# Where the last two column groups fetch their input rows, and which queue moves them: a state-space convolution block with a gated bilinear network on one core

## The chip, the cores and the metric

One core of one Trainium2 chip runs the kernel. The metric is device time in microseconds (us), from one launch; the figure given is the median of three runs. One further execution of the same program was taken with the hardware profiler on, and every time that is read from a trace below belongs to that one execution.

## The reference

The input x is one sequence of 2048 tokens with 640 features, float32. Cut to what matters:

```python
mod = (silu(c) @ w_mod)                       # sa, ca, ga, sb, cb, gb: six rows of 640
h = layernorm(x) * (1 + ca) + sa
x = x + ga * S4(h)                            # a causal convolution over the 2048 tokens, one filter per feature, by FFT, plus h * Dskip
h = layernorm(x) * (1 + cb) + sb
x = x + gb * (((h @ w_gate) * (h @ w_up)) @ w_down)   # 640 -> 1536 -> 640
```

The filter of a feature is a sum over 192 complex states of C * exp(dt*A*l) * B.

## The kernel before, in words

The 640 features are five column groups of 128 (`db` 0 to 4, `NB` = 5). The 2048 tokens are seen as 128 partitions of 16 tokens, and the 16 are four quarters of four (`c` 0 to 3), so that one token block is 128 x 4 = 512 tokens. The kernel has two parts.

The first part (to about 500 us in the profile) makes the filters (matmuls into the tile `kg`), transforms filters and inputs (`u_k`, `u_pre`, `u_g`), multiplies them in the frequency domain and goes half the way back (`u_c`, which stores its result in the DRAM tensor `WD`, one per column group, through the two buffers `Wa` and `Wb`), and goes the rest of the way back in `u_d`. For one column group and one quarter, `u_d` loads the piece of `WD` into a buffer `TVa` or `TVb` (two transfers of 256 KB) and the input columns of x into a buffer `xsa` or `xsb` (256 KB in runs of 512 bytes), runs four matmuls into a PSUM tile, adds the input to it on VectorE, and stores the sum to the DRAM tensor `x2d` (256 KB). All of these transfers are issued by SyncE (SP), the stores of `WD` at the end by ScalarE.

The second part is the network. It starts with token blocks 0 and 1 (quarters 0 and 1), whose sums are also kept in SBUF, in the tiles `xb0` and `xb1` (128 x 4 x 640, `XB` in the code). `rows` loads columns 0 to 383 of such a block back from `x2d`; for the last two column groups, `u_d` writes its sum straight into the kept tile. `u_head` then takes the statistics of the layernorm (`bn_stats` on VectorE, tile `a`), the factors `hr`, the normalized pieces `hf` (half of each on ScalarE, half on GpSimd), their transposes on TensorE, and the split of these into two float32r parts `hh` and `hl`. From there on the matmuls of the network run (`prod`, the lines of `pa` and `psg`) to the end of the kernel. Thirty and then four matmuls with no use of their result (`warm`) stand where TensorE would have no work ahead of `u_head`.

Every engine works through its own list in order, and so does the list of transfers that an engine issues. The order of the lists is written out: `SCHED` gives, for each step of each job (`d` for `u_d`, `c` for `u_c`, `w` for weight loads, `wl` for `rows`, `h` for `u_head`), a place in one common count from about -1000 to 2880, and `due` runs the steps as the count goes by. A job is a generator; each `yield` ends a step. `SLOT` says by a letter for each allocation which of two or three buffers of a ring (`TV`, `xs`, `hf`, `psf`) it takes. A transfer into a buffer waits until the readers of its former content are done, and each transfer that SP or ScalarE issues also waits for the one that used the same semaphore, eight transfers back.

Of the kernel before, what the change touches and what calls it, by code (L numbers as in the profile page):

```python
# [14 lines left out]
OP = mybir.AluOpType  # L15
# [79 lines left out]
            (2433, 2608, 2608, 2648, 2679, 2703),  # L95
            (2425, 2484, 2537, 2554, 2645, 2677),
            (2477, 2493, 2636, 2656, 2680, 2719),
            (2387, 2439, 2532, 2545, 2620, 2633),
# [48 lines left out]
        (2461, 2497),  # L147
        (2497, 2510),
    ),
    low=(168, 419, 677, 899, 1101, 1385, 1631, 1857, 2075),  # L150
    w=(2478, 2613, 2684, 2668, 2879, 2879),
    wl=(2590, 2441),
    wm=(2732, 2755),
    h=(2709, 2738, 2775, 2811, 2843, 2843, 2857, 2875),
# [6 lines left out]
    ),  # L161
)
# [5 lines left out]
    TV="baabababaabbaabbbabbaababbaababbaabbabbaababab",  # L168
# [3 lines left out]
    hf="abacbcabacbacabcbacccacaabbcbaacabaabbabcaccababbcbbacaabcabbcbba",  # L172
    psf="cacabccbcaccbabbaacbbcacabacbcbacacbbaacabbcabcabcbacbbcbcbcababccbacabcabacbacbaccacbacbaccababbcabcabcabbcabcabcacacab"
    "cbcbaacbacbacbabccabcaacabcaabcbcabcabccabcabcbbacbcbacbacbacbacbacbbabccabacbaacbcabcbacabcabcabcabcababcacbabcacbaacbc"
    "abaabcabcacbacbacacbacbacaaacacbcaba",
    tr="bbababababababababababababababababababababababbabbabababaababbaaababababababababababababababababbbabbababaababababbabbbb"
    "a",
    xs="aabababbabaaabababab",
# [51 lines left out]
def tile_kernel(ctx: ExitStack, tc: tile.TileContext, I, out):  # L230
# [46 lines left out]
    def need(n, *k):  # L277

        assert done.get(k, 0) >= n, k
# [695 lines left out]
    def u_d(db, c):  # L975
        need(4, "WD", db)
        Vt = ring(fp, [P, 2, 4, P], "TV")
        v = WD[db].rearrange("(b t q h) k d -> (q h k) t b d", t=2, q=2, h=2)
        for h in range(2):
            SY.dma_start(Vt[:, h], v[:, h, 4 * c : 4 * c + 4])  # L980
        xs = ring(fp, [P, 4, P], "xs")
        SY.dma_start(xs, xin[:, 4 * c : 4 * c + 4, db * P : db * P + P])
        yield
        d0 = slice(db * P, db * P + P)
        ps = ring(PF[-1], [P, 4, P], "psf")
        for q in range(4):
            lo = q % 2 * 64
            PE.matmul(ps[32 * q : 32 * q + 32], t_ib[lo : lo + 64], Vt[lo : lo + 64, q // 2], start=True, stop=True, tile_position=(lo, 32 * q))
        yield
        mark("d", c)  # L990
        if db >= NB - 2 and c < 2:
            V.tensor_tensor(XB[c][:, :, d0], ps, xs, op=OP.add)
            xs = XB[c][:, :, d0]
        else:
            V.tensor_tensor(xs, ps, xs, op=OP.add)
        SY.dma_start(x2d[:, 4 * c : 4 * c + 4, d0], xs)
# [357 lines left out]
    for t in range(3 * NK + 24):  # L1354
# [17 lines left out]
        if t == 3 * NK + 1:  # L1372
# [519 lines left out]
```

## Time and profile before

| | |
|---|---|
| three runs | 964.3, 961.07, 963.75 us, median 963.75 |
| the profiled execution | 962.34 us, span 960.6 us from its first to its last instruction |
| mean granted TensorE clock | 0.989 |
| busy share of the span | TensorE 93%, VectorE 73%, ScalarE 60%, GpSimd 49% |
| bytes moved | 188.59 MB, 196 GB/s over the span |

The span leaves out 1.74 us of the profiled execution's own time, around the first and the last instruction. In the profile a row of the timeline gives start and length in us, the engine, the source line and the tiles (out<-in); in square brackets stands how long the engine had been idle before the row and what ended that. SPq and ACTq are transfers issued by SyncE and ScalarE; their length is that of the issue, not of the transfer.

### The profile page before, as it was taken

The numbers are of one execution on the slowest core, as the hardware profiler recorded it, in microseconds if no ns is written. First come the engines' busy times: TensorE is split into PE (matmuls) and PEld (weight loads), VectorE is DVE, ScalarE is ACT, GpSimd is POOL, SyncE is SP. The second block draws the span as 40 slices with busy tenths as digits, with TensorE's granted clock in tenths as the row PEclk, the third lists the DMA queues.
The fourth block names the chain that finished last, engine by engine and source line by source line (L and its number), as shares of the span: only waits on it lengthen the run. The fifth ranks groups of instructions, "written<-read, shape, count | busy, mean of one in ns | idle before, by whom it ended". The sixth has DMA issues, their size and how long they took to land.

```text
span 960.6 us, 27559 instructions
## 1 busy us (share of the span) xinstructions
PE 892.6 (93%) x11646; PEld 734.0 (76%) x11646; DVE 705.6 (73%) x1250; ACT 580.5 (60%) x1016; POOL 471.2 (49%) x369
## 2 busy tenths in 40 slices
PE   1898787999899899998889999999999999999998
PEld 1675555878776677887558888889999788888997
DVE  8977888878888986767688555557585766569952
ACT  6989999887988977763276333234463543435430
POOL 3998997986699668750041345320013323231110
PEclk9989999999999999999999999999999999999999
DMA  7876546435267646547894675435536576758875
GB/s 238 324 243 242 186 131 199 146 108 153 78 207 197 187 124 194 184 128 228 277 308 152 192 246 192 165 140 172 200 120 196 171 238 208 244 172 289 253 231 189
DMA packets 158819, 188.59 MB, mean 196 GB/s; under 512 B 9828, under 2 KB 128360, under 8 KB 157544
## 3 DMA queue, kind: packets, MB, share of 16 engines
q1 hardware_dynamic: 149480, 155.51, 50.3%
q0 software_dynamic: 4752, 21.63, 7.8%
q10 hardware_dynamic: 4464, 9.70, 2.7%
q8 instruction: 91, 1.49, 0.6%
q14 instruction: 32, 0.26, 0.1%
HBM read 124.22 MB, written 62.59 MB: 194 GB/s over the span
## 4 chain that ended last, share of the span: by engine, by line
PE 61%; ACT 12%; issue 10%; DVE 7%; POOL 5%; DMA 4%; SPq 0%; POOLq 0%; DVEq 0%; ACTq 0%
PE pa L1095 19%; PE psg L1095 9%; PE pa L1527 7%; PE kg L825 3%; PE kg L840 2%; PE psfa L907 2%; PE psfb L967 2%; PE psfb L907 2%; ACT L235 2%; PE psfc L967 1%; PE psfc L907 1%; PE psfa L967 1%; PE psfc L886 1%; ACT trb L235 1%; ACT tra L235 1%
## 5 line engine op out<-in xcount | busy, mean ns | idle before, releaser
L1072 POOL TENSOR_TENSOR tf<-wur,wgb 128x256 f32<-128x256 f32 x23 | 17.5, 760 | 241.5 <-DVE wtl L1043 193.2
L729 POOL TENSOR_TENSOR EQ<-LQ,RH 128x1536 f32<-128x1536 f32 x40 | 114.8, 2870 | 5.3 <-DVE QtB L785 5.3
L1043 DVE TENSOR_TENSOR wtl<-tf,wth 128x256 fp32r<-128x256 f32 (+1 forms) x72 | 37.0, 516 | 59.2 <-ACT wth L235 59.2
L729 POOL TENSOR_TENSOR Phb<-LH,DH 128x1536 int32<-128x1536 int32 x21 | 60.3, 2871 | 32.6 <-ACT trb L235 19.3
L729 POOL TENSOR_TENSOR EP<-LP,RH 128x768 f32<-128x768 f32 x40 | 61.9, 1547 | 1.7 <-ACT RH L235 1.7
L729 POOL TENSOR_TENSOR Pha<-LH,DH 128x1536 int32<-128x1536 int32 (+1 forms) x20 | 54.1, 2703 | 9.2 <-ACT trb L235 8.5
L1527 PE MATMUL pa<-wsg,sh 128*128 128x384 f32 (+1 forms) x304 | 58.1, 309 | 0.0
L840 PEld LDWEIGHTS kg<-QtB,PtB 64*32 64x32 f32 x2560 | 38.3, 108 | 13.4 <-issue 6.9
L1043 DVE TENSOR_TENSOR wsg<-wga,wsg 128x640 fp32r<-128x640 f32 x36 | 35.5, 988 | 14.8 <-ACT wsg L235 14.8
L840 PE MATMUL kg<-QtB,PtB 64*32 64x64 f32 x2560 | 44.6, 219 | 1.8 <-DVE QtB L785 1.8
L1527 PEld LDWEIGHTS pa<-wsg,sh 128*128 128x128 f32 x304 | 45.4, 188 | 0.0
L1566 POOL DMA_DIRECT2D wsg<-wdc x21 | 11.2, 532 | 66.6 <-PE pa L1579 35.7
L235 ACT ACTIVATE sh<-a 128x512 fp32r<-128x512 f32 x55 | 33.3, 626 | 13.9 <-PE psg L1579 6.2
L1043 DVE TENSOR_TENSOR sl<-a,sh 128x512 fp32r<-128x512 f32 x55 | 38.0, 710 | 3.9 <-ACT sh L235 3.9
L235 ACT ACTIVATE wsg<-wga 128x640 fp32r<-128x640 f32 x36 | 26.2, 731 | 23.7 <-PE pa L1527 12.6
L1095 PE MATMUL pa<-hh,wsg 128*128 128x512 f32 x150 | 40.0, 393 | 0.0
L235 ACT ACTIVATE a<-pa 128x512 f32<-128x512 f32 x12 | 7.2, 596 | 49.9 <-PE pa L1095 49.9
L235 ACT ACTIVATE s<-pa 128x512 f32<-128x512 f32 x12 | 7.2, 598 | 49.2 <-PE pa L1095 47.0
L235 ACT ACT_TABLE_LOAD x25 | 32.1, 1283 | 7.2 <-DMA pta<-A_A_re 4.2
L784 DVE TENSOR_TENSOR QtA<-trb,EQ 128x1024 f32<-128x1024 f32 x22 | 26.8, 1216 | 11.9 <-POOL EQ L729 4.4
L235 ACT ACTIVATE wth<-tf 128x256 fp32r<-128x256 f32 (+1 forms) x72 | 32.4, 481 | 4.5 <-DVE tf L1073 1.8
L1527 PE MATMUL pa<-wsg,sl 128*128 128x384 f32 (+1 forms) x152 | 34.5, 308 | 0.0
(672 smaller groups left out, 3230.0 us busy)
## 6 DMA issues: line engine op xcount, KB each, us to landing
wsg<-wdc POOLq DMA_DIRECT2D x21, 640.0 KB, 5.1
wgb<-B_w_gate SPq DMA_DIRECT2D x24, 320.0 KB, 4.1
wur<-B_w_up SPq DMA_DIRECT2D x24, 320.0 KB, 5.6
wsd<-wsg SPq DMA_DIRECT2D x12, 640.0 KB, 3.7
wga<-wdg SPq DMA_DIRECT2D x12, 640.0 KB, 3.9
wsg<-wsd POOLq DMA_DIRECT2D x12, 640.0 KB, 4.8
wdc<-xb SPq DMA_DIRECT2D x21, 320.0 KB, 4.5
TVb<-WD SPq DMA_DIRECT2D x26, 256.0 KB, 3.5
```

The lines of the kernel that those rows point to most:

```text
L235: return S.activation(o, i, f, **kw)
L729: G.tensor_tensor(o.rearrange("p x (h l) -> p x h l", l=8), lo.unsqueeze(2).to_broadcast([P, rows, nh, 8]), hi.unsqueeze(3).to_broadcast([ ...
L784: return [lambda: V.tensor_tensor(Qt[:, :, :, 0:32], tr[:, :, :, ::-1], e[:, :, 0:32].unsqueeze(1).to_broadcast([P, 2, R, 32]), op=OP.mult ...
L825: PE.matmul(kg[j * 32 : j * 32 + 32, dd, :], PtA[:, c, dl * 4 + j, :], QtA[:, c, dl * 4 + j, :], start=dd == 0 and c == 0, stop=False, til ...
L840: PE.matmul(kg[j * 32 : j * 32 + 32, dd, :], PtB[lo : lo + 64, c, r, :], QtB[lo : lo + 64, c, r, :], start=False, stop=dd == 7 and c == 1, ...
L907: PE.matmul(r[c][par * 64 : par * 64 + 64, i, :], t_tw[:, k0 + k, c, :], src[:, k, :], start=True, stop=True, tile_position=(0, par * 64))
L967: PE.matmul(r[par][:, i], t_ti[lo : lo + 64, qd * 4 + i, c, :], y[lo : lo + 64, i, :], start=k == 0, stop=k == len(x) - 1, tile_position=( ...
L1043: V.tensor_tensor(lo, v, hi, op=OP.subtract)
L1072: E.tensor_tensor(t[:, 0:2], u[:, 0:2], g[:, 0:2], op=OP.subtract)
L1095: PE.matmul(ps, w[a][:, k], x[b][:, l], start=first and n == 0 and m == 0, stop=n == 2 and m == len(ks) - 1, skip_group_check=True)
L1527: PE.matmul(AC[tb][t][c], x[:, ts], w[:, cs], start=st, stop=f == NF - 1 and n == 2 and (c == 0 or t % 2 == 1))
L1566: G.dma_start(WD[q], wdc[:, q // 3, q % 3])
```

## The change

For the last two column groups (`db` 3 and 4) the transfers of `u_d` are rearranged in three ways, and the tail's places are set anew.

- Token blocks 0 and 1: the input columns 384 to 639 are loaded by SP in one transfer for each block (512 KB, runs of 1 KB), straight into the kept tile (`kept_l`, at the places `xl`), ahead of the sums. `u_d` then adds in place, and there is no load into `xs`. The sums of both groups go to `x2d` in one transfer (512 KB) once the second is there.
- Token blocks 2 and 3: the loads into `xs` stay, but GpSimd issues them.
- All stores to `x2d` for these two groups are issued by GpSimd.
- The places of the last jobs in `SCHED` and the letters in `SLOT` move with it. In all, SP's list goes from 365 to 351 rows and GpSimd's from 336 to 346.

```diff
-    w=(2478, 2613, 2684, 2668, 2879, 2879),
-    wl=(2590, 2441),
+    w=(2551, 2649, 2616, 2708, 2874, 2879),
+    wl=(2636, 2655),
...
+    xl=(2496, 2569),
...
     def u_d(db, c):
         need(4, "WD", db)
+        Q = G if db >= NB - 2 else SY
         Vt = ring(fp, [P, 2, 4, P], "TV")
...
-        xs = ring(fp, [P, 4, P], "xs")
-        SY.dma_start(xs, xin[:, 4 * c : 4 * c + 4, db * P : db * P + P])
+        d0 = slice(db * P, db * P + P)
+        kept = db >= NB - 2 and c < 2
+        if not kept:
+            xs = ring(fp, [P, 4, P], "xs")
+            Q.dma_start(xs, xin[:, 4 * c : 4 * c + 4, d0])
         yield
-        d0 = slice(db * P, db * P + P)
         ps = ring(PF[-1], [P, 4, P], "psf")
...
         mark("d", c)
-        if db >= NB - 2 and c < 2:
-            V.tensor_tensor(XB[c][:, :, d0], ps, xs, op=OP.add)
+        if kept:
+            need(1, "xl", c)
             xs = XB[c][:, :, d0]
-        else:
-            V.tensor_tensor(xs, ps, xs, op=OP.add)
-        SY.dma_start(x2d[:, 4 * c : 4 * c + 4, d0], xs)
+        V.tensor_tensor(xs, ps, xs, op=OP.add)
+        if kept:
+            mark("kept", c)
+            if done["kept", c] < 2:
+                return
+            d0, xs = LAST, XB[c][:, :, LAST]
+        Q.dma_start(x2d[:, 4 * c : 4 * c + 4, d0], xs)
...
+    LAST = slice((NB - 2) * P, NB * P)
...
+            def kept_l(tb):
+                SY.dma_start(XB[tb][:, :, LAST], xin[:, 4 * tb : 4 * tb + 4, LAST])
+                mark("xl", tb)
...
+                at(T0["xl"][j : j + 1], once(kept_l), j)
```

What that does to the lists shows best on SP. Here is its list before, from the load of column group 3's third quarter on (`A_u` is the input x, `wga` a weight buffer, `xb_6999` is xb0):

```order
L980 DMA TVb<-WD 128x4x128 x2
L982 DMA xsb<-A_u 128x4x128
L980 DMA TVa<-WD 128x4x128 x2
L982 DMA xsa<-A_u 128x4x128
L1021 DMA wga_7266<-B_w_gate 128x5x256
L996 DMA x2d<-xsa 128x4x128
L996 DMA x2d<-xsb 128x4x128
L980 DMA TVb<-WD 128x4x128 x2
L982 DMA xsb<-A_u 128x4x128
L980 DMA TVa<-WD 128x4x128 x2
L982 DMA xsa<-A_u 128x4x128
L996 DMA x2d<-xb_6999 128x4x128
```

And SP's list at the same place after the change (`xb_7002` is xb0, `xb_7003` is xb1):

```order
L1396 DMA xb_7002<-A_u 128x4x256
L982 DMA TVb<-WD 128x4x128 x2
L1030 DMA wga_7177<-B_w_gate 128x5x256
L1396 DMA xb_7003<-A_u 128x4x256
L1393 DMA xb_7002<-x2d 128x4x384
L982 DMA TVa<-WD 128x4x128 x2
L1030 DMA wga_7317<-B_w_gate 128x5x256
L1393 DMA xb_7003<-x2d 128x4x384
L982 DMA TVb<-WD 128x4x128 x2
L982 DMA TVa<-WD 128x4x128 x2
L1030 DMA wga_7405<-B_w_gate 128x5x256
L982 DMA TVb<-WD 128x4x128 x2
```

The loads of `xs` and the stores to `x2d` have left the list; the load of `TVb` for column group 4's first quarter (the eighth row before, the ninth now) stands behind a weight load and a load of kept rows in place of two stores. Before, the piece of GpSimd's list where the filters end and `u_head` begins had no transfer in it:

```order
L729 TENSOR_TENSOR EQ_141<-LQ_144,RH_151 128x1536
L729 TENSOR_TENSOR EP_143<-LP_147,RH_151 128x768
L1165 TENSOR_SCALAR hfb<-xb_6999,hr_7432,hr_7433 128x128 x2
L1165 TENSOR_SCALAR hfc<-xb_6999,hr_7432,hr_7433 128x128 x2
L1165 TENSOR_SCALAR hfb<-xb_6999,hr_7432,hr_7433 128x128 x4
L1165 TENSOR_SCALAR hfa<-xb_6999,hr_7432,hr_7433 128x128 x2
L1176 TENSOR_SCALAR xb_7000<-xb_7000,hr_7530,hr_7531 128x640
```

After the change GpSimd's list reads so at that place:

```order
L987 DMA xsb<-A_u 128x4x128
L1004 DMA x2d<-xsb 128x4x128
L987 DMA xsa<-A_u 128x4x128
L987 DMA xsb<-A_u 128x4x128
L1004 DMA x2d<-xsa 128x4x128
L1004 DMA x2d<-xb_7002 128x4x256
L1174 TENSOR_SCALAR hfa<-xb_7002,hr_7429,hr_7430 128x128 x2
L1174 TENSOR_SCALAR hfc<-xb_7002,hr_7429,hr_7430 128x128 x2
L1004 DMA x2d<-xsb 128x4x128
L1174 TENSOR_SCALAR hfc<-xb_7002,hr_7429,hr_7430 128x128 x2
L1004 DMA x2d<-xb_7003 128x4x256
L1174 TENSOR_SCALAR hfb<-xb_7002,hr_7429,hr_7430 128x128 x4
```

Six transfers now stand ahead of the first normalized piece and two between the pieces; two more follow behind them.

More of the change, by code (lines that the diff above doesn't have):

```diff
@@ L94 @@
         (
[L95 to L98, printed above, removed]
+            (2427, 2551, 2551, 2568, 2620, 2635),
+            (2427, 2452, 2510, 2524, 2615, 2622),
+            (2463, 2481, 2591, 2595, 2633, 2657),
+            (2397, 2410, 2500, 2521, 2567, 2620),
         ),
@@ L146 @@
         (2344, 2352),
-        (2461, 2497),
-        (2497, 2510),
+        (2461, 2470),
+        (2469, 2476),
     ),
     low=(168, 419, 677, 899, 1101, 1385, 1631, 1857, 2075),
-    w=(2478, 2613, 2684, 2668, 2879, 2879),
-    wl=(2590, 2441),
-    wm=(2732, 2755),
-    h=(2709, 2738, 2775, 2811, 2843, 2843, 2857, 2875),
+    w=(2551, 2649, 2616, 2708, 2874, 2879),
+    wl=(2636, 2655),
+    wm=(2660, 2757),
+    h=(2624, 2661, 2771, 2792, 2820, 2832, 2850, 2872),
     g=(
@@ L167 @@
     PtA="abababababababababababababababbabaababba",
-    TV="baabababaabbaabbbabbaababbaababbaabbabbaababab",
+    TV="ababababaabbaabbbabbaababbaabababaaabaaaababab",
     W="abbbbbabababbbbabbaabbaba",
@@ L171 @@
     gh="cbacbacbcacbacbacbbcbcacbabccaabcabacba",
-    hf="abacbcabacbacabcbacccacaabbcbaacabaabbabcaccababbcbbacaabcabbcbba",
+    hf="abacbcabacbacabcbacccacaabbcbaacabaabbabcaccababbcbbacaabcabaccbb",
     psf="cacabccbcaccbabbaacbbcacabacbcbacacbbaacabbcabcabcbacbbcbcbcababccbacabcabacbacbaccacbacbaccababbcabcabcabbcabcabcacacab"
     "cbcbaacbacbacbabccabcaacabcaabcbcabcabccabcabcbbacbcbacbacbacbacbacbbabccabacbaacbcabcbacabcabcabcabcababcacbabcacbaacbc"
-    "abaabcabcacbacbacacbacbacaaacacbcaba",
+    "abcabcabcacbacbacacbacbacbaacbcacaba",
     tr="bbababababababababababababababababababababababbabbabababaababbaaababababababababababababababababbbabbababaababababbabbbb"
     "a",
-    xs="aabababbabaaabababab",
+    xs="aabababbabababab",
 )
```

8 rows, old and new, of tables (d, g) are left out of this document.

## The prediction

> **What bounds the kernel now.** I read the page's busy shares and its chain of waits first, then a table of windows around the place of the change, then the chain piece by piece. The page, and the windows (us from the span's start; busy time and count for each engine; granted clock; busy share of the DMA engines; GB/s):
>
> ```profile
> PE 892.6 (93%) x11646; PEld 734.0 (76%) x11646; DVE 705.6 (73%) x1250; ACT 580.5 (60%) x1016; POOL 471.2 (49%) x369
> ...
> PE 61%; ACT 12%; issue 10%; DVE 7%; POOL 5%; DMA 4%; SPq 0%; POOLq 0%; DVEq 0%; ACTq 0%
> ```
>
> ```profile
> 454.00:457.00 3.00, 2.32 (x56) 2.13 (x56) 2.79 (x8) 1.12 (x3) 0.00 (x0) 1.00 0.04 13
> 457.00:470.00 13.00, 10.21 (x126) 7.39 (x123) 4.76 (x10) 5.98 (x9) 0.00 (x0) 1.00 0.97 320
> 470.00:478.00 8.00, 8.00 (x39) 5.60 (x38) 7.06 (x35) 0.00 (x0) 0.00 (x0) 1.00 0.76 231
> 478.00:500.00 22.00, 19.00 (x102) 10.16 (x100) 18.10 (x47) 13.11 (x26) 9.78 (x15) 1.00 0.98 300
> ```
>
> ```profile
> 500.00:960.00 460.00, 455.72 (x2404) 402.41 (x2402) 300.70 (x545) 188.87 (x362) 116.43 (x138) 1.00 0.61 200
> ```
>
> From 500 us on TensorE is busy 455.72 of 460 us; what is gained before the network's matmuls start comes through to the end one for one, and nothing else in the change touches that part. The room is ahead of it. Between 457 and 478 us VectorE and ScalarE are half idle while the DMA engines are full (0.97), and TensorE's 8.00 of 8 in 470 to 478 are mostly matmuls without use. The chain there, by start, length and what it is:
>
> ```profile
> 461.72 7.58 DMA xsa<-A_u
> ...
> 470.00 0.69 DVE xsb L995
> ...
> 470.70 4.03 DMA x2d<-xsb
> ...
> 474.75 2.96 DMA xsb<-A_u
> ...
> 477.80 0.70 DVE xb L992
> ```
>
> So the last add into token block 0, at 477.80, is released by the load of its input columns; the load waited for the store that emptied its buffer, the store for an add, the add for another input load. These are the transfers that the change moves. That row at 477.80 is the gate: the statistics of block 0 follow it at once, and `u_head` hangs on them. But other work ends just ahead of it, and that decides the sum:
>
> ```profile
> 464.31 0.38 PE L967 MATMUL psfa<-f16a,t_ti 64*128 64x128 f32 x2
> 466.46 1.42 PE L988 MATMUL psfc<-TVa,ct 64*32 64x512 f32 x6 [1.76 <-DMA TVa<-WD]
> ...
> 469.10 7.09 PE L1196 MATMUL psg<-wsg 128*128 128x512 f32 x30
> 476.12 1.32 PE L988 MATMUL psfa<-TVb,ct 64*32 64x512 f32 x8
> ```
>
> ```profile
> 460.40 0.33 ACTq L972 DMA_DIRECT2D WD<-Wa  x1
> ...
> 466.55 0.60 ACT L235 ACTIVATE Wa<-psfb 128x512 f32<-128x512 f32 x1 [3.47 <-DMA WD<-Wa]
> ...
> 467.67 0.33 ACTq L972 DMA_DIRECT2D WD<-Wa  x1
> ```
>
> ```profile
> 472.14 0.91 SPq L980 DMA_DIRECT2D TVb<-WD  x2
> ```
>
> ```profile
> SPq L996 <- DVE xsa L995: 5.7, 1, 5.7
> ...
> SPq L980 <- DMA WD<-Wa: 0.8, 1, 0.8
> ```
>
> The second chain: TensorE ends the last `u_c` at 464.69; ScalarE wants to copy it into `Wa` but waits 3.47 us until the former content has left (460.40 to about 466.5, 6.1 us for 512 KB); the last store goes at 467.67; SP waits for it last (0.8 us, to 472.14, so it took 4.4 us) and only then loads `TVb`; the matmuls on it end at 477.44. SP's 5.7 us behind the add of `xsa` were over before 470.70, when it issued the second of its two stores, and the `WD` store landed later: SP's blocked list was a wait, but not the last one. Taking away the load of `xsb` alone therefore moves the gate by 477.80 - 477.44 = 0.36 us and no more. VectorE is the third: its 32 statistics ran to 476.86.
>
> ```profile
> 470.59 6.27 DVE L1156 BATCH_NORM_STATS2 a<-xb 128x6 f32<-128x128 f32 x32
> ```
>
> **The change part by part.** *Input loads of the kept blocks* (four of 256 KB become two of 512 KB, with about twice the run length, issued near 438 and 447 us by my reading of SP's list): worth the 0.36 us above, if nothing else moves. Their cover is the early place; if it went, the add would wait about 3 us (the 2.96 row). The four adds now work in place, one instruction of 0.7 us each as before: 0.
>
> *DMA load between 457 and 470.* Before, 456.6 to 467.7 us issue four `WD` stores (2048 KB), `TVb` and `TVa` (1024 KB), two input loads (512 KB) and a weight load (640 KB), 4224 KB, and two stores follow. After, SP's list has `TVb`, one input load and the first weight load at about 446, where the DMA engines have room (0.04 in 454 to 457), and at 460 `TVa` (512 KB), the second weight load (640 KB) and the late kept rows (768 KB): with the `WD` stores 3968 KB, plus 512 KB that GpSimd issues from 466 on. So about as many bytes, but the queue that the second `WD` store meets at 460.40 is nearly empty instead of 768 KB deep, and after 467.7 SP's queue is almost drained. The store that took 6.1 us and the last one at 4.4 us can fall to 3.2 us, the median of the page's row for the same transfer on SP:
>
> ```profile
> WD<-Wa SPq DMA_DIRECT2D x6, 512.0 KB, 3.2
> ```
>
> Bounds: 0, if the bytes in flight set it, to 1.8 + 1.2 us; the first is capped at 1.8 (466.55 to TensorE's end at 464.69). I take 0.4 for the first, since the loads that SP issues at 460 still run beside it, and 0.9 for the second, near the light price, since by then SP's queue is nearly done. With the 0.36 us: 1.7 us. A cap comes from the others: VectorE's order is now add, add, 32 statistics, a weight split (1.0, row below), an add, then the gate's add. From the matmuls on `TVb`, which need not wait for `TVa` any more (464.7 + 1.1), that is 465.8 + 0.7 + 6.3 + 1.0 + 0.7 = 474.5, if the kept rows of block 1 have landed by 469.7, 8 us after their issue. TensorE's unused matmuls then run 466.8 to 473.9. So the gate can't come before about 475.3 with its matmuls (1.3 us), which caps the gain at 2.5 us.
>
> ```profile
> L1043 DVE TENSOR_TENSOR wsg<-wga,wsg 128x640 fp32r<-128x640 f32 x36 | 35.5, 988 | 14.8 <-ACT wsg L235 14.8
> ```
>
> *SP's list.* It loses 14 issues, of 0.3 to 0.9 us by the rows above, all off the chain, as shown: 0. Behind the late `TVb` stands a weight load that waits for a VectorE split now; it is needed after 500 us: 0.
>
> *VectorE's buffers.* All of `u_c`'s products now use `TVa`, so three more of them wait for the instruction before on the same engine. The rows show what that costs: with such a wait 0.10 us between end and start, without one an overlap of 0.1:
>
> ```profile
> 446.23 0.41 DVE L956 TENSOR_TENSOR f16a<-TVa,psfb 128x256 f32<-128x256 f32 x1
> 446.56 0.68 DVE L992 TENSOR_TENSOR xb<-psfa,xsa 128x512 f32<-128x512 f32 x1
> ...
> 449.22 0.42 DVE L956 TENSOR_TENSOR ghc<-TVb,psfc 128x256 f32<-128x256 f32 x1
> 449.74 0.69 DVE L946 TENSOR_TENSOR TVb<-psfb,ghb 128x512 f32<-128x512 f32 x1
> ```
>
> Two of them lie ahead of the `Wa` copies, 0.1 to 0.2 us each: 0.3 us lost. ScalarE now makes the high part of the first weight split ahead of its copy to `Wb`:
>
> ```profile
> 455.46 0.60 ACT L235 ACTIVATE Wb<-psfa 128x512 f32<-128x512 f32 x1 [3.03 <-PE psfc L967]
> ```
>
> ```profile
> wga<-B_w_gate SPq DMA_DIRECT2D x3, 640.0 KB, 7.5
> ```
>
> Its weights, issued near 447 and landing in 7.5 us as before, are there at 454.5, just in time: 0, at most 0.8 lost.
>
> *GpSimd's transfers.* Ten new ones, four loads and six stores. Before, its transfers have 128 long runs, these have 512:
>
> ```profile
> L1052 POOL DMA_DIRECT2D wsg<-wsd x12: 527/568/797, 720.5 to 831.0; - x12
> ...
> DMA to landing us min/median/max: 4.1/4.8/8.1
> ```
>
> ```profile
> 481.85 0.88 POOL L1165 TENSOR_SCALAR hfb<-xb,hr,hr 128x128 f32<-128x128 f32 x2 [54.71 <-DVE hr L290]
> ...
> 483.58 0.87 POOL L1165 TENSOR_SCALAR hfb<-xb,hr,hr 128x128 f32<-128x128 f32 x2
> ```
>
> ```profile
> 485.13 0.83 PE L1186 MATMUL psfb<-ident,hfb 128*128 128x128 f32 x4
> ```
>
> ```profile
> 487.47 0.80 DVE L1188 TENSOR_SCALAR a<-psfb,colT 128x512 f32<-128x512 f32 x1
> ```
>
> ```profile
> 495.04 0.74 POOL L1072 TENSOR_TENSOR tf<-wur,wgb 128x256 f32<-128x256 f32 x1 [2.36 <-issue]
> ```
>
> A price from 0.53 us (the shortest) to 3.2 us (the longest, 0.80, four times for four times the runs). The store of `xb0` sits between the gate's add and the first pieces, which start 3.4 us after that add's end (478.50 to 481.85): covered up to there. The store of `xsb` holds up the third piece; its transposes start 0.68 us after it is done (484.45 to 485.13). At 1.1 us, twice the short price, that is 0.4 us late for TensorE, and VectorE takes the transposes only at 487.47, 1.5 us after their end; I take the price near the measured row and charge 0.2 for the pieces behind. The bounds are 0 and 2.5 (3.2 - 0.68). Behind the last piece, a load of `xsb` and a store that waits for its add stand ahead of the sums on GpSimd that ran from 495.04 before. They feed matmuls after 500 us, where TensorE has had other work throughout (the 500 to 960 row): 0; without that cover, the 4 to 5 us until that load has landed and been added.
>
> A rule of the Trainium skill speaks against the move: DMA: Bandwidth & Descriptors, "Issuing engines are not separate DMA queues", says that transfers from several engines end up on the same 16 DMA engines, so that more issuers save only issue time. Here the row of SP's 5.7 us wait shows that a list can also be blocked, which is more than issue time; that it was not the last wait agrees with the rule's result. By the rule the move off SP is worth 0.
>
> The sum: -0.4 -0.9 -0.36 +0.3 +0.2 = -1.2 us, so 962.34 - 1.2 = 961.1 us for an execution like the profiled one. That execution lies 1.4 us below the median of the runs, 963.75; a median is what will be compared, so 962.5 us.
>
> **The rivals.** *Hidden anyway.* The same bytes go over the same engines and the last `WD` store lands when it did; the gate moves by 0.36 us and VectorE and GpSimd give 0.5 back: 963.9. For it: 0.97 busy from 457 to 470, and about as many bytes after. Against it: the idle 454 to 457.
>
> *All of the cap, and a shorter head.* Both `WD` stores at the light price give the 2.5 us, and the 22 us from 478 to 500, where the DMA engines stand at 0.98 and TensorE idles 3.0 us, give 1 more: 960.3. For it: GpSimd's own queue takes eight transfers out of SP's. Against it: none of the waits in that stage's chain is a transfer.
>
> *GpSimd becomes the bound (slower).* Each of its new transfers holds it for 3.2 us. The third piece comes 2.5 us late, of which VectorE's 1.5 us take a part; the fourth stands behind one more store, so 3.2 us later again; and the last load of `xsb` lands 3.2 us later, with VectorE's work behind it. Some 4 to 5 us against 1.7 gained: 963.75 + 2.3 to 3.3, about 966.5. It decides from about 1.4 us a transfer on. For it: no transfer of this form is in the trace. Against it: the short ones cost 0.53. SBUF: State Buffer of the Trainium skill, the box on the "DVE blocks DMA" trap, tells of such a transfer at 3100 ns instead of 620 beside a VectorE copy; no run here shows that, and by its 2.5 us more for each the sum would be this rival's.
>
> **How the numbers follow.** The forecast (gain of 0.3 to 2.5 us) 0.5, hidden anyway 0.14, cap and head 0.17, GpSimd the bound 0.19. A measurement of this kernel can tell about 0.3% (2.9 us) from no change, since three runs of one program spread over 3.2 us. Faster by more than that: the cap rival and a share of the forecast's upper end, 0.25. Slower: most of the GpSimd rival, 0.16. The rest, 0.59, the same. The range: from 963.75 - 2.5 - 2 for a low median, 959.3, to the slow rival, 966.6.
>
> **What would show it.** In the profile after: the last add into xb0 (start) at 475.3 to 477.5 and released by TensorE, not by a load; ScalarE's wait ahead of the last `Wa` below 3.47 us; `TVb` for the first quarter of group 4 issued before 472.1; GpSimd's transfers at 0.5 to 1.1 us each, and TensorE without new waits for GpSimd between 478 and 500. I am wrong if the `WD` stores take as long as before (then: hidden), or if rows of GpSimd's transfers of 2 us and more stand between the normalized pieces.

## The result and the profile after

| | before | after |
|---|---|---|
| median of the runs | 964.02 us (961.07 to 968.02, 4 runs) | 975.19 us (973.99 to 976.33, 4 runs) |
| ratio after to before | | 1.0124, 95% interval 1.0094 to 1.0154 |
| the profiled execution, its span | 962.34, 960.6 | 974.52, 972.7 |
| mean granted TensorE clock | 0.989 | 0.972 |

The changed kernel is slower, by 11 us; 962.5 us was forecast. The page's busy line, and the table of windows around the place of the change (same columns as before):

```profile
PE 899.6 (92%) x11646; PEld 738.3 (76%) x11646; DVE 704.6 (72%) x1250; ACT 581.0 (60%) x1016; POOL 477.7 (49%) x379
```

```profile
457.00:470.00 13.00, 10.73 (x112) 7.89 (x108) 6.46 (x23) 5.28 (x8) 0.78 (x1) 1.00 0.81 284
470.00:478.00 8.00, 4.68 (x22) 3.03 (x22) 4.60 (x18) 0.00 (x0) 1.51 (x2) 0.86 0.67 179
478.00:500.00 22.00, 14.24 (x48) 5.71 (x43) 11.69 (x39) 5.38 (x13) 7.15 (x12) 0.50 0.79 253
```

Over these 43 us together every engine is less busy than before (TensorE 29.7 us instead of 37.2, VectorE 22.8 instead of 29.9), though TensorE and VectorE do a little more in the first window; the DMA engines do less in all three, 0.81, 0.67 and 0.79 where they stood at 0.97, 0.76 and 0.98. So engines wait, and the sum of their work has not grown. TensorE has 102 matmul records in 478 to 500 before, 48 now, at a clock of 0.50.

To compare kernels I measure one stretch of TensorE's list: from the end of the last `u_c` matmul (line 967 before, 968 after) to the start of the network's first product into `pa` (line 1095, now 1104). What lies ahead of it varies by some us between executions of kernels that are the same there; what lies behind it took 460.64 us before and 460.35 after. The row that ends it before, then both rows of after:

```profile
499.96 1.17 PE L1095 MATMUL pa<-hh,wsg 128*128 128x512 f32 x4
```

```profile
462.92 0.38 PE L968 MATMUL psfa<-f16a,t_ti 64*128 64x128 f32 x2
...
512.35 1.18 PE L1104 MATMUL pa<-hh,wsg 128*128 128x512 f32 x4
```

Before: 499.96 - 464.69 = 35.27 us. After: 512.35 - 463.30 = 49.05 us, 13.78 more. With 1.39 gained ahead of the stretch and 0.29 behind it that is the 12.1 us by which the spans differ. Of the 13.78, 3.23 lie ahead of the gate (13.11 us into the stretch before, 16.34 now), 10.55 between the gate and the network.

**Ahead of the gate.** Rows of SP, ScalarE, TensorE and VectorE of the kernel after, each list by itself:

```profile
459.94 2.23 SPq L1393 DMA_DIRECT2D xb<-x2d  x1
472.34 0.91 SPq L982 DMA_DIRECT2D TVb<-WD  x2
```

```profile
465.94 0.33 ACTq L973 DMA_DIRECT2D WD<-Wa  x1
```

```profile
476.88 2.71 PE L992 MATMUL psfa<-TVb,ct 64*32 64x512 f32 x8 [3.32 <-DMA TVb<-WD]
```

```profile
470.41 3.19 DVE L1165 BATCH_NORM_STATS2 a<-xb 128x6 f32<-128x128 f32 x16 [2.26 <-DMA xb<-x2d]
...
475.99 0.69 DVE L998 TENSOR_TENSOR xsa<-psfb,xsa 128x512 f32<-128x512 f32 x1 [1.67 <-DMA xsa<-A_u]
479.64 0.69 DVE L998 TENSOR_TENSOR xb<-psfa,xb 128x512 f32<-128x512 f32 x1 [2.96 <-PE psfa L992]
```

The last `WD` store is issued earlier (465.94, before 467.67), but `TVb` can be loaded only at 472.34: the store took up to 6.4 us, 4.4 before; SP's list stood for 10.1 us at that point, and what it waited for last was this store. Beside it runs the 768 KB load of block 1's finished rows, issued at 459.94; that load is itself late for the statistics (2.26 us). The gate is released by TensorE, as said, but at 479.64.

**Between the gate and the network.** GpSimd's transfers, and its first normalized piece:

```profile
465.47 0.78 POOL L1004 DMA_DIRECT2D x2d<-xsb  x1 [39.38 <-DVE xsb L998]
471.82 0.76 POOL L987 DMA_DIRECT2D xsa<-A_u  x1 [5.57 <-issue]
476.20 0.75 POOL L987 DMA_DIRECT2D xsb<-A_u  x1 [3.62 <-issue]
482.14 0.76 POOL L1004 DMA_DIRECT2D x2d<-xsa  x1 [5.20 <-DVE hr L284]
486.60 0.76 POOL L1004 DMA_DIRECT2D x2d<-xb  x1 [3.70 <-issue]
487.40 0.88 POOL L1174 TENSOR_SCALAR hfa<-xb,hr,hr 128x128 f32<-128x128 f32 x2
...
492.68 0.80 POOL L1004 DMA_DIRECT2D x2d<-xsb  x1 [3.54 <-DVE xb L998]
497.67 0.80 POOL L1004 DMA_DIRECT2D x2d<-xb  x1 [3.27 <-DVE hr L284]
502.32 0.81 POOL L987 DMA_DIRECT2D xsb<-A_u  x1
```

Each transfer holds GpSimd for 0.75 to 0.81 us. But ahead of each of the next six stand 3.3 to 5.6 us of idle time that the profile calls "issue", or puts down to a VectorE row that the transfer has no use for (the store of `xsa` needs the add that ended at 476.68, not `hr`). The starts of the eight rows, 465.47 to 502.32, lie 5.26 us apart on average. The trace also gives each transfer's time from issue to landing, here for the first four, one by one:

```profile
x2d<-xsb POOLq DMA_DIRECT2D x1, 256.0 KB, 6.0
...
xsa<-A_u POOLq DMA_DIRECT2D x1, 256.0 KB, 4.1
...
xsb<-A_u POOLq DMA_DIRECT2D x1, 256.0 KB, 5.6
...
x2d<-xsa POOLq DMA_DIRECT2D x1, 256.0 KB, 4.2
```

The next row starts 6.35, 4.38, 5.94 and 4.46 us after the start of each of these, so each time about 0.3 us after the landing. The next two fit as well: landings after 5.8 and 4.7 us, next rows after 6.08 and 4.99. So GpSimd starts a transfer only when the one before has landed. And its normalized pieces stand behind the transfers: `hfa` at 487.40 where `hr` was ready at 483.5. TensorE waits for GpSimd three times:

```profile
487.91 0.91 PE L1195 MATMUL psfc<-ident,hfa 128*128 128x128 f32 x3 [3.34 <-POOL hfa L1174]
494.04 0.90 PE L1195 MATMUL psfa<-ident,hfc 128*128 128x128 f32 x3 [1.98 <-POOL hfc L1174]
499.06 0.69 PE L1195 MATMUL psfc<-ident,hfb 128*128 128x128 f32 x2 [1.35 <-POOL hfb L1174]
```

### The profile page after: what moved, and what is told of

It reads as the page before. It is cut to its first block, busy times and chain, and to the rows that moved or that the text cites. A ratio compares the mean times of both kernels' runs of the same rounds, so it can differ in the third digit from the quotient of the medians.

```text
span 972.7 us, 27559 instructions
## 1 busy us (share of the span) xinstructions
PE 899.6 (92%) x11646; PEld 738.3 (76%) x11646; DVE 704.6 (72%) x1250; ACT 581.0 (60%) x1016; POOL 477.7 (49%) x379
## 4 chain that ended last, share of the span: by engine, by line
PE 64%; ACT 11%; DVE 9%; issue 8%; POOL 4%; DMA 3%; POOLq 0%; DVEq 0%; SPq 0%; ACTq 0%
PE pa L1104 20%; PE psg L1104 9%; PE pa L1541 7%; PE kg L826 3%; PE kg L841 3%; PE psfa L908 2%; PE psfc L908 2%; PE psfb L968 2%; PE psfb L908 2%; PE psfc L968 2%; ACT L236 1%; PE psfc L887 1%; PE psfa L968 1%; PE psfb L887 1%; PE psfa L863 1%
## 5 line engine op out<-in xcount | busy, mean ns | idle before, releaser
L1580 POOL DMA_DIRECT2D wsg<-wdc x21 | 11.2, 532 | 66.5 <-PE pa L1593 35.4
```

## The experiments

The theory, **A**: GpSimd writes the descriptors of its transfers into a scratch of SBUF, of which the kernel reserves 1024 bytes per partition (`dynamic_dma_scratch_size`). A transfer of 512 runs fills more than half of it, so the next one waits on GpSimd until the last has landed. DMA: Bandwidth & Descriptors of the Trainium skill says under "Terms" that a descriptor has 16 bytes and that GpSimd's path writes them to rings in SBUF, and under "The descriptor swizzle" counts one more per DMA engine for the completion. An estimate worked out from that page's figures: a transfer of 512 runs needs 32 + 1 on each of the 16 engines, and 1024 bytes hold 64, not 66; the GpSimd transfers of before, with 128 runs, need 8 + 1. Rivals: **B**, GpSimd is slow to write these transfers beside VectorE or on full DMA engines; **C**, the tail's new order costs the time, whoever issues.

All times "to the gate" and "to the network" are counted from the start of the stretch above, in the one profiled execution of that kernel. The medians stand beside the medians of the kernel before on the same chip.

| run | edit | median (before beside it) | ratio, 95% interval | to the gate | to the network |
|---|---|---|---|---|---|
| | before | | | 13.11 | 35.27 |
| | after | 975.19 (964.02) | 1.0124, 1.0094 to 1.0154 | 16.34 | 49.05 |
| 1 | memory freed, scratch 1024 | 984.32 (961.64) | 1.0218, 1.0179 to 1.0256 | 15.01 | 50.24 |
| 2 | same, scratch 2048 | 973.15 (961.64) | 1.011, 1.0079 to 1.0141 | 17.58 | 43.72 |
| 3 | all on SP | 971.85 (961.64) | 1.0101, 1.006 to 1.0143 | 17.61 | 42.75 |
| 4 | only stores on GpSimd | 976.76 (961.64) | 1.0148, 1.011 to 1.0185 | 15.37 | 47.26 |
| 5 | rows early | 973.93 (964.19) | 1.0097, 1.0074 to 1.0121 | 13.84 | 48.74 |
| 6 | scratch 2048, rows early | 973.01 (964.19) | 1.0093, 1.0066 to 1.0119 | 11.66 | 37.75 |
| 7 | before, kept rows alone | 966.89 (964.19) | 1.0038, 1.0018 to 1.0058 | 12.70 | 34.69 |
| 8 | all on SP, rows early | 972.6 (963.04) | 1.0103, 1.0066 to 1.014 | 17.37 | 44.60 |
| 9 | as 6, loads on SP | 971.8 (963.04) | 1.0083, 1.0057 to 1.0109 | 11.89 | 37.56 |
| 10 | more unused matmuls | 978.87 (963.04) | 1.0167, 1.0137 to 1.0198 | 15.32 | 47.88 |
| 11 | four stores on GpSimd, rows early, TVb ahead | 964.23 (962.38) | 1.0015, 0.999 to 1.004 | 11.19 | 34.55 |
| 12 | as 11, TVb behind | 965.68 (962.38) | 1.0033, 1.0012 to 1.0055 | 11.71 | 37.11 |
| 13 | as 1, scratch 1088 | 973.39, one run (968.01, one run) | | 15.20 | 41.38 |
| 14 | as 1, scratch 1536 | 977.75, one run (968.01, one run) | | 16.63 | 43.07 |

**1 and 2: the scratch.** SBUF is full, so room is made first (the same in both; run 1, at 984 us instead of the 973 to 977 expected, is 9 us slower than the changed kernel, and its stretch starts 8.8 us later, so run 1 is what run 2 is to be held against): the scratch tile `prm` of the filters' seeds is folded into `ptb` and `pta`, and ten small tiles of the first part move to a pool that closes early.

```diff
-        prm = pk1.tile([P, 2, N], F32, name="prm")
-        rho, f, amp = prm[:, 0, :], prm[:, 1, :], prm[:, 0, :]
-        x, u, y, v = tb_[:, 0, :], tb_[:, 1, :], ta[:, 1, :], ta[:, 1, :]
+        rho, f, amp = ta[:, 0, :], ta[:, 1, :], tb_[:, 0, :]
+        x, u, y, v = tb_[:, 0, :], ta[:, 1, :], tb_[:, 1, :], ta[:, 1, :]
...
-    nc = bacc.Bacc(..., dynamic_dma_scratch_size=1024)
+    nc = bacc.Bacc(..., dynamic_dma_scratch_size=2048)    # the second kernel only
```

> Control for the next kernel: only the seeds' scratch tile prm is folded into the other two, and small tiles of the first stage move to a pool that closes early; the descriptor scratch stays at 1024 bytes per partition. Theory A (a GpSimd transfer of 512 runs needs 32 descriptors on each of the 16 DMA engines, the scratch of 1024 bytes has 64, so the next transfer waits on GpSimd until the last has landed): 973 to 977 us, as the changed kernel, with the same 3 to 6 us gaps ahead of GpSimd's transfers. Theories B (GpSimd's transfers are slow to write beside VectorE or on full DMA engines) and C (the tail's new order of jobs costs the time): the same.

> As the control, with 2048 bytes of descriptor scratch per partition, 128 descriptors, so that three such transfers fit. Theory A: the gaps named issue ahead of GpSimd's transfers, 3.3 to 5.6 us each, go below 0.5 us; the load of xsa starts near 467 instead of 471.8; TensorE's waits for hfa, hfc and hfb go; clock 1.00 again from 480 to 500; 960 to 965 us. Theory B: gaps and time as in the control, 973 to 977. Theory C: the gaps go, the gate stays at 479 or later and the clock at about half from 480 to 500; 968 to 975.

GpSimd's transfers with 1024 bytes, then with 2048:

```profile
481.25 0.76 POOL L987 DMA_DIRECT2D xsa<-A_u  x1 [6.21 <-issue]
486.70 0.75 POOL L987 DMA_DIRECT2D xsb<-A_u  x1 [4.69 <-issue]
492.93 0.76 POOL L1004 DMA_DIRECT2D x2d<-xsa  x1 [5.48 <-issue]
```

```profile
469.06 0.77 POOL L1004 DMA_DIRECT2D x2d<-xsb  x1 [39.18 <-DVE xsb L998]
469.82 0.76 POOL L987 DMA_DIRECT2D xsa<-A_u  x1
476.10 0.76 POOL L987 DMA_DIRECT2D xsb<-A_u  x1 [5.52 <-DMA x2d<-xsb]
```

With the larger scratch the load of `xsa` follows the store of `xsb` at once, and the load of `xsb` after it waits for a store that its buffer needs. Nothing else differs between the two programs: B is out, and A holds. The stretch falls by 6.5 us, from 50.24 to 43.72. The medians differ by 11.2 us, but in the profiled executions 5.1 us lie ahead of the stretch. The granted clock from 100 to 200 us differs there, 0.91 in run 1 and 0.98 in run 2; but run 13 below has 0.98 too, and its stretch starts 2.9 us later than run 2's, so the clock is not all of it. I give the scratch the 6.5 and leave the rest open.

But 960 to 965 us was expected, and 43.72 is still 8.5 us above 35.27, 4.5 of them ahead of the gate. The median of 973.15 and the late gate are what C's expectation had (968 to 975 us); only the clock, 0.84 over 478 to 500 us, is not at the half that went with it. So A is not all of it; something in the tail's new order costs time as well.

**13 and 14: how much room.** The page counts packets by queue; GpSimd's before and after:

```profile
q0 software_dynamic: 4752, 21.63, 7.8%
```

```profile
q0 software_dynamic: 5680, 24.78, 8.6%
```

The 928 more, for eight transfers of 256 KB and two of 512 KB, are 64 + 16 packets of 4 KB for 256 KB, where SP's queue lost 7392 for 14 transfers, 512 + 16 each. So the packets don't show 33 descriptors per DMA engine, and that count was only argued. Two more sizes of the scratch, otherwise run 1 again:

```diff
-    nc = bacc.Bacc(..., dynamic_dma_scratch_size=1024)
+    nc = bacc.Bacc(..., dynamic_dma_scratch_size=1088)    # run 13; 1536 in run 14
```

> As the first two kernels of the study, with 1088 bytes of scratch, 68 descriptors of 16 bytes. Theory A33 (a transfer of 512 runs takes 32 + 1 descriptors on each DMA engine, two take 66): two fit now, so the load of xsa follows the store of xsb without a gap (under 0.5 us), as with 2048 bytes. Theory A-not-33 (the transfer takes more than 34, or the scratch counts in steps of 1024 bytes): the gap of 4 to 6 us stays, as with 1024.

> The same with 1536 bytes, 96 descriptors. Theory A33: no gap ahead of the load of xsa, as with 2048. If the scratch counts in steps of 1024 bytes or a power of two: the gap of 4 to 6 us stays. If a transfer takes 35 to 48 descriptors: a gap with 1088 bytes, none here.

With 64 bytes more the gap is gone:

```profile
471.97 0.77 POOL L1004 DMA_DIRECT2D x2d<-xsb  x1 [39.07 <-DVE xsb L998]
472.73 0.77 POOL L987 DMA_DIRECT2D xsa<-A_u  x1
```

The stretch runs from 469.91 to 511.29 with 1088 bytes and from 469.55 to 512.62 with 1536: 41.38 and 43.07 us, beside 43.72 with 2048 and 50.24 with 1024. So two such transfers fit into 1088 bytes and not into 1024, as 33 descriptors of 16 bytes each would have it (34 would fit too; the 32 of run 1's expectation would have let two into 1024). That the trace packs eight runs into a packet doesn't change what the scratch must hold. By these runs the scratch is worth 6.5 to 8.9 us of the stretch. The three kernels with room enough show no gap of this kind and still lie 2.3 us apart, with the gate at 15.20 to 17.58, so smaller differences between single executions, such as some further down, prove nothing by themselves.

**3: all back on SP.**

```diff
-        Q = G if db >= NB - 2 else SY
+        Q = SY
```

> The changed kernel with GpSimd's ten transfers given back to SP; the early kept rows and the tail's new order of jobs stay. Theory A: no gaps on GpSimd, clock 1.00 from 480 to 500, gate at 476 to 478; 960 to 965 us. Theory B: the same, 960 to 965. Theory C: still slow, 968 to 975.

42.75 us, which fits C's numbers; but the trace shows another reason. In SP's list the store of `xsb` stands ahead of block 1's rows, and it must wait for VectorE's add at 466.26. So the rows go at 470.08, and the statistics wait 7.81 us:

```profile
470.08 1.03 SPq L1393 DMA_DIRECT2D xb<-x2d  x1
```

```profile
477.85 3.19 DVE L1165 BATCH_NORM_STATS2 a<-xb 128x6 f32<-128x128 f32 x16 [7.81 <-DMA xb<-x2d]
```

The order of the lists and the issuing engine belong together, so this run can't judge the order alone. It points to the load of the rows, as the trace of after does.

**4: only the stores on GpSimd.**

```diff
-            Q.dma_start(xs, xin[:, 4 * c : 4 * c + 4, d0])
+            SY.dma_start(xs, xin[:, 4 * c : 4 * c + 4, d0])
```

> The changed kernel with the three input loads (xsa, xsb, xsb) given back to SP; only the six stores stay on GpSimd. Theory A: the gate is freed (476 to 478.5, since the load of xsa no longer waits behind the store of xsb), but stores that follow each other within 4 us still stall, so the second and fourth piece of the head still come 2 to 4 us late: 964 to 971 us. Theory B: six of ten transfers are left, 968 to 972. Theory C: 970 to 975.

The stretch is 1.8 us shorter than after's; the median of 976.76 was not expected by any theory, and its stretch starts 4.2 us later than after's. Of A's expectation, the gate (15.37 us in, so 1 us earlier) came in part, and the head stalled far more than the 2 to 4 us that I gave it. The stores in the head are still 5 to 6.5 us apart, with gaps of this kind:

```profile
494.61 0.81 POOL L1004 DMA_DIRECT2D x2d<-xsb  x1 [3.58 <-DVE xb L998]
...
499.84 0.81 POOL L1004 DMA_DIRECT2D x2d<-xb  x1 [3.51 <-DVE hr L286]
```

**5 and 6: block 1's rows early, without and with room in the scratch.** Theory **D**: the late load of the rows is a second cause. One number of the schedule, so that SP issues this load ahead of the weights and of the `WD` stores, as before the change (run 6 also has the edits of run 2):

```diff
-    wl=(2636, 2655),
+    wl=(2590, 2441),
```

> The changed kernel with one transfer moved: the 768 KB load of block 1's finished rows goes back to where it stood before the change, ahead of the weights and of the last WD stores (447 us instead of 459.9). Theory A+D (beside the full GpSimd scratch, this late load runs against the last WD store and comes late for the statistics): last WD store lands 1.5 to 2.5 us earlier, so TVb of group 4 goes 7 to 7.5 us after the last u_c matmul instead of 9.0; the statistics of block 1 no longer wait 2.3 us; the gate comes 13.5 to 15 us after the last u_c matmul instead of 16.3 (the load of xsa behind the full scratch holds it there); GpSimd's gaps in the head stay: 971 to 974 us. Theory A alone: no difference, 973 to 977.

> 2048 bytes of scratch and block 1's finished rows loaded early, both at once. Theory A+D: from the last u_c matmul to the gate 13 to 14.5 us (17.6 with the larger scratch alone), from there to the network's first matmul 24 to 26; 3 to 4 us below the larger scratch alone: 968 to 971 us. A rival, E (the gate and the head are late because TensorE runs at half clock after its idle time, whatever the loads do): gate still beyond 16.5 us, time as with the larger scratch alone, 972 to 974.

Run 5 does at the gate what D says: the last `WD` store has landed 4.3 us after its issue (6.4 in after), `TVb` goes 6.36 us into the stretch instead of 9.04, no wait of the statistics, gate 2.5 us earlier. And at the network only 0.3 us are left of it, less than these executions can tell, since GpSimd's transfers still come one by one and the pieces behind them:

```profile
480.44 0.75 POOL L987 DMA_DIRECT2D xsb<-A_u  x1 [5.45 <-issue]
```

```profile
490.34 0.90 PE L1195 MATMUL psfc<-ident,hfa 128*128 128x128 f32 x3 [4.71 <-POOL hfa L1174]
```

With room in the scratch the same edit takes the stretch from 43.72 to 37.75 us: 6.0 us. The gate comes at 11.66, below the 13 to 14.5 expected and 1.45 us better than before the change; with room and late rows it came at 15.20 to 17.58 (runs 2, 13, 14). The medians don't show the 6 us: 968 to 971 was expected, and run 6 stands at 973.01, 0.1 us below run 2, or 8.8 us above its kernel before where run 2 stood 11.5 above. In the profiled executions 1.8 us of the difference lie ahead of the stretch and 1.3 behind it; the rest is open. What is left over before, 2.5 us, is in the head: 26.1 us from the gate to the network, 22.2 before. The stretch of run 6 by its ends, then GpSimd and TensorE in the head:

```profile
468.43 0.38 PE L968 MATMUL psfa<-f16a,t_ti 64*128 64x128 f32 x2
...
506.56 1.17 PE L1104 MATMUL pa<-hh,wsg 128*128 128x512 f32 x4
```

```profile
496.94 0.88 POOL L1185 TENSOR_SCALAR xb<-xb,hr,hr 128x640 f32<-128x640 f32 x1 [3.79 <-DMA x2d<-xb]
```

```profile
497.77 1.75 PE L992 MATMUL psfa<-TVb,ct 64*32 64x512 f32 x8 [1.31 <-DMA TVb<-WD]
...
503.96 1.53 PE L1195 MATMUL pa<-ident,xb 128*128 128x128 f32 x12 [1.46 <-DVE xsb L998]
```

**7: the kept rows alone, in the kernel before.** `kept_l` and the joint store as in the change, all on SP, in before's schedule, with places for the two loads:

```diff
+    xl=(2480, 2440),
```

> The kernel before with one part of the change alone: the input rows of the last two column groups go straight into the kept token rows, early, and leave in one store for both groups; all transfers stay on SP and the order of the jobs is that of before. From the prediction: 0.36 us at the gate, so 961 to 964 us for a kernel before of 962 to 964, and the gate released by TensorE or VectorE instead of the load of xsb. If this part itself is harmful (its 512 KB loads or stores run against the last WD stores): 965 or more.

The gate moves by -0.41 us (0.36 forecast) and the stretch by -0.58, both less than two executions can differ by. Still the kernel is 2.7 us slower by the medians, in the range given for a harmful part: my two 512 KB loads go at 437.47 and 439.46, and VectorE's first add into block 1 (at 440.50 before) now waits for one, with `u_c`'s products queued behind it.

```profile
444.27 0.69 DVE L998 TENSOR_TENSOR xb<-psfa,xb 128x512 f32<-128x512 f32 x1 [7.83 <-DMA xb<-A_u]
```

That add starts 3.8 us later than before. So in that order of VectorE's list the early loads are not early enough; the change gives those adds later places, and the load no longer stands ahead of them as a wait (444.91 and 459.05 us, neither with idle time ahead).

**8 and 9: who should issue.** Run 8 is run 5 with `Q = SY`; run 9 is run 6 with the loads on SP (the edit of run 4).

> The changed kernel with block 1's finished rows loaded early and all ten of GpSimd's transfers given back to SP, scratch 1024: what is left of the change are the kept rows and the tail's order. Theory A+D: no full scratch, no late rows, and SP's stores no longer hold up the rows: from the last u_c matmul to the gate 12 to 13.5 us, to the network's first matmul 35 to 38 us (before 35.3, changed 49.0): 962 to 967 us. If GpSimd's issuing was needed for the order to work (SP blocked behind the stores, as in the run with everything on SP): 41 us or more to the network, 968 to 972.

> 2048 bytes of scratch, block 1's rows early, and the three input loads on SP, the six stores on GpSimd. Theory F (what is left over before, 2.7 us to the network's first matmul, comes from the order of GpSimd's list: the last load of xsb stands behind the in-place normalisation of block 1, which waits 3.8 us for that block's store): the 1.5 us wait of the transposes of xb for the add of xsb goes; 36 to 37 us to the network instead of 38.0; 970 to 973 us. Rival G (TVb's last load behind 1.3 MB of weights on SP sets it): that wait stays and the time as with the loads on GpSimd, 37.5 to 38.5 us to the network.

Run 8 turned out as the last sentence of its expectation has it: 44.60 us to the network. SP's list is blocked by one store that waits for VectorE; `TVa` is loaded behind it, TensorE waits for `TVa`, and then 30 unused matmuls (7.5 us) stand in its list ahead of the gate's:

```profile
464.32 0.37 SPq L1004 DMA_DIRECT2D x2d<-xsb  x1
464.73 1.51 SPq L982 DMA_DIRECT2D TVa<-WD  x2
```

```profile
468.70 2.69 PE L992 MATMUL psfb<-TVa,ct 64*32 64x512 f32 x8 [5.17 <-DMA TVa<-WD]
471.33 7.52 PE L1205 MATMUL psg<-wsg 128*128 128x512 f32 x30
```

So GpSimd's list does free SP's, for this store. Run 9 gains 0.2 us over run 6, within what executions differ by, and the wait for the add of `xsb` falls from 1.46 to 0.95: theory F is at most a small part, and G stays.

**10: more unused matmuls**, to keep TensorE's clock up.

```diff
-            at(T0["wm"][0:1], once(warm), 30)
-            at(T0["wm"][1:2], once(warm), 4)
+            at(T0["wm"][0:1], once(warm), 44)
+            at(T0["wm"][1:2], once(warm), 18)
```

> The changed kernel with 14 more unused matmuls of TensorE in each of its two idle stretches (ahead of TVb's last matmuls in front of the gate, and ahead of the first transposes), so that it does not fall to half clock. If half clock is a cause of its own (rival E): the matmuls from 480 to 503 run at 1.06 us for eight instead of 1.93, and 2 to 4 us are won: 971 to 973. If it only follows from the waits (theory A): clock up, but the time within 1 us of the changed kernel's, 974 to 977.

```profile
478.00:500.00 22.00, 14.32 (x68) 7.40 (x66) 10.71 (x34) 5.02 (x13) 5.72 (x10) 0.92 0.86 262
```

The clock is at 0.92 in this window instead of 0.50, and from gate to network it takes 32.56 us instead of 32.71. So the half clock cost nothing from the gate to the network that the waits did not cost already. (The median is 3.7 us above after's, above both ranges of the expectation; the profiled execution has 3.5 us more ahead of the stretch, and the stretch itself is 1.2 shorter.)

**11 and 12: a version that avoids all of it.** After, with the scratch of 1024, rows early, and

```diff
-            Q.dma_start(xs, xin[:, 4 * c : 4 * c + 4, d0])
+            SY.dma_start(xs, xin[:, 4 * c : 4 * c + 4, d0])
...
-            d0, xs = LAST, XB[c][:, :, LAST]
+            Q, d0, xs = SY, LAST, XB[c][:, :, LAST]
...
-        ..., (2736, 2816, 2816), (2835, 2851, 2879), (2699, 2715, 2783)),
+        ..., (2736, 2816, 2816), (2819, 2851, 2879), (2699, 2715, 2783)),    # run 11 only
```

> The changed kernel, scratch 1024, with four edits: block 1's finished rows early; the three input loads and the two 512 KB stores of the kept rows on SP; so GpSimd keeps only the four 256 KB stores, which lie 7 us and more apart and never meet in the scratch; and TVb's last load ahead of the four weight loads on SP. Theory A+D+G: GpSimd's transfers without a gap named issue, from the last u_c matmul to the gate 11.5 to 12.5 us, to the network's first matmul 34 to 36 us (before 35.3): 961 to 966 us. If what is left over came from GpSimd's 0.8 us holds or from the tail's order itself: 37 us or more, 967 to 972.

> The same without the last edit: TVb's last load stays behind the four weight loads. Theory G (that order costs the head): 1 to 2 us more than with TVb ahead, 36 to 37.5 us from the last u_c matmul to the network, with a wait of TensorE for TVb of about 1 us and of the transposes of xb for the add of xsb: 963 to 968 us. If the order of these loads doesn't matter: within 0.5 us of its sibling to the network.

```profile
466.15 0.38 PE L968 MATMUL psfa<-f16a,t_ti 64*128 64x128 f32 x2
...
501.08 1.17 PE L1104 MATMUL pa<-hh,wsg 128*128 128x512 f32 x4
```

Run 11 needs 34.55 us, 0.72 less than before the change (less than two executions can differ by), and its four transfers on GpSimd have no gap named issue. Run 12 has `TVb`'s last load behind four weight loads and TensorE waits for it, 2.6 us of stretch for one number of the schedule:

```profile
496.03 1.83 PE L992 MATMUL psfa<-TVb,ct 64*32 64x512 f32 x8 [2.54 <-DMA TVb<-WD]
```

By the medians run 11 can't be told from the kernel before (1.0015, 0.999 to 1.004); 0.7 us is less than these runs can show. Against the change as made it wins the 11 us back; the kernel before is not beaten.

## Why the prediction was wrong

The stretch comes apart in this order: room in the scratch 6.5 (runs 1 and 2), block 1's rows early 6.0 (2 and 6), loads off GpSimd 0.2 (6 and 9), the 512 KB stores off GpSimd 0.45 (9 and 12, which also goes back to the small scratch), `TVb` ahead of the weights 2.6 (12 and 11). Their sum is 15.7 us, from run 1's 50.24 (after's 49.05, in the memory layout with room) to 34.55, just below the 35.27 of before. The shares depend on the order: run 5 shows that the rows are worth 0.3 while the scratch is full. They are differences of single executions, which can differ by 2.3 us for no such reason; the two of 0.2 and 0.45 can't be told from nothing, and what carries the three large ones is that in the trace the named wait goes with each.

- **GpSimd's transfers, +0.2 forecast.** This is the step that failed most. I priced a transfer by the row of its instruction (0.53 to 3.2 us, taken 1.1), and the rows came out at 0.75 to 0.81, inside what I had said would show me right. The cost is not in that row. It stands ahead of the next transfer, where that one's turn comes before the last has landed (4.1 to 6.0 us after its issue), and it came to 6.5 us of the stretch. Nothing in the trace of before showed it, since there no GpSimd transfer has 512 runs; my bounds from "a price per transfer" left out a price per pair. The slower rival had the right place and the wrong mechanism: 3.2 us for each of a few transfers, against 5.26 us from one to the next, eight in a row. "Covered up to there" (the store of `xb0` ahead of the first pieces) failed too: `hfa` started 3.9 us after `hr`.
- **The last WD store, -0.9 forecast.** It took 6.4 us, +2.0, and I had written that a store as slow as before would show me wrong. I counted "about as many bytes" and left out when they run: the rows at 459.94 share the DMA engines with it. Even with the rows early it takes 4.3 (run 5), 3.9 (run 6) and 4.7 us (run 11), never the 3.5 that I took, near the 3.2 of the page's median for SP.
- **The cap and its condition.** "If the kept rows of block 1 have landed by 469.7": the statistics on them began at 470.41, after 2.26 us of waiting, with the add of `xsa`, 1.67 us late from GpSimd, behind them. These rows took 10.5 us from their issue to the first statistics on them, where I had 8. I had named the condition and given it no price.
- **SP's list, 0 forecast.** The issues taken away were off the chain, as said. But I looked at the weight load behind the late `TVb`, and not at the four weight loads now ahead of another one in the head: 2.6 us, once the scratch no longer hides it.
- **Right:** the gate freed from the load of `xsb` (TensorE releases it), and the first weight split at 0 (ScalarE waited 1.64 us for the weights, and its copy to `Wb` still waited 0.66 for TensorE after it). VectorE's +0.3 for the single `TVa` is not to be seen: the last `u_c` matmul ended 1.39 us earlier than before, for reasons not followed up. The gain at the gate that the sum aimed at, 1.7 us less 0.3, is there when the two causes are away: 1.45 us in run 6, 1.92 in run 11, within the cap of 2.5.
- **The second WD store, -0.4 forecast: right in the number, in part by luck.** ScalarE's wait went from 3.47 to 3.13 us, -0.34. But from the issue of the store ahead to the end of that wait it took 5.96 us, after 6.15: the store was hardly faster, and nowhere near 3.2. The rest of the 0.34 comes from its issue, which lies 4.44 us ahead of the end of `u_c` instead of 4.29.
- **The Trainium skill's rule** on issuing engines (DMA: Bandwidth & Descriptors) gave 0 for the move off SP. Runs 8 and 12 differ only in who issues the four 256 KB stores, SP or GpSimd: 44.60 against 37.11 us, since a list that waits for VectorE holds up what stands behind it. More than issue time is at stake, in both directions. The 3100 ns that SBUF — State Buffer of the Trainium skill tells of ("A bandwidth-pool intuition that's wrong (but worth ruling out)"), for a transfer beside a copy on VectorE, were not seen; no row of a GpSimd transfer of 512 runs exceeds 1.02 us.

What stays open: why the part ahead of the stretch differs by some us between kernels (its end lies between 462.5 and 469.9 us, and at 472.1 in run 1); this is as large as the effects in question, and the medians follow the stretch only loosely. The clock granted early on differs between runs 1 and 2, but run 13 shows that it is not all of it. Where run 6 loses what its stretch gains over run 2 is open too.

## What to carry to other kernels

Before moving transfers to GpSimd, count the runs of each and what may be in flight together against the descriptor scratch: the duration of one row says nothing about the second transfer, and whatever compute stands behind it on GpSimd waits as well. When a change moves several loads, ask of each late one what it now runs beside, and what it now stands ahead of in its list; byte totals of a window don't tell. An idle time that the profile calls "issue" ahead of one kind of instruction, as long as that kind takes to land, was here the sign of a resource that was full.

## What the hardware showed that was not expected

- A GpSimd transfer of 512 runs waits, with 1024 bytes of scratch, until about when the one before has landed (2.3 to 6.2 us of idle time ahead of a row of 0.76, in the changed kernel and runs 1 and 5); with 1088 it follows at once. Perfetto Trace Analysis of the Trainium skill ("DMA Instruction — SWDGE (GPSIMD)") says that such a row ends when the descriptors are written; here the wait for room lies outside the row as well, ahead of it.
- TensorE's granted clock fell to 0.50 over 478 to 500 us when it had little to do (48 matmul records instead of 102), and eight matmuls that take 1.06 us took 1.93; filling its idle time brought a clock of 0.92, and less than 0.2 us from the gate to the network.
